# A new table of durations, a term for changes of matmul kind and other begin and due times in the planner of a linear-attention and MLP kernel

## The chip, the cores and the metric

The kernel runs on one core of one Trainium2 chip. The metric is device microseconds (us) of one execution. Of the kernel before, three runs were timed; one more execution was taken by the hardware profiler, and everything read from a trace comes from that one.

## What is computed

The input is four arrays `r`, `k`, `v`, `w` of shape (4 batches, 8 heads, 768 tokens, 48 channels), a vector `u` per head, and the two weights of an MLP. All is float32. The attention is a recurrence over tokens with a 48x48 state per head:

```python
for t in range(S):
    cur = np.einsum('bhd,bhe->bhde', u[None] * kt, vt)
    y[:, :, t] = np.einsum('bhd,bhde->bhe', rt, state + cur)
    state = wt[:, :, :, None] * state + np.einsum('bhd,bhe->bhde', kt, vt)
```

The 8 heads of `y` are put side by side (384 columns, 3072 tokens). Then comes the MLP: `h = x @ w_in` (384 by 2048), an ELU, and `@ w_out` (2048 by 384).

## The kernel before

**Tiling.** The 768 tokens are cut into 6 chunks of 128. A chunk of one batch is a *unit*, so there are 24 units, numbered chunk by chunk: units 0 to 3 are chunk 0. The four units of a chunk give the 512 columns of one MLP pass. Chunks 2 to 4 (units 8 to 19) treat each unit as two half chunks of 64 tokens.

**Attention of a unit i.** Names in brackets are those of the planner. SyncE (SP) loads w, k, r, v and, from unit 8 on, rk (`ld_...`). VectorE (DVE) runs two scans over the decays (`es` L377, `gs` L387) and multiplies them into r and k (`rh` L392, `kh` L396). TensorE (PE) computes scores (`s` L456), transposes k (`t` L465), multiplies values (`v` L501, or L493 and L506 in half chunks), forms the outer product for the state (`u` L532) and, for half chunks, the part of the first half that comes from the state (`ya` L506). The diagonal term with `u` goes for units 0 to 7 through DVE (`rkc` L416), PE (`pd` L421) and ScalarE (ACT: the copy `md` L425, then eight instructions `sp` L432 that write the diagonal matrices); from unit 8 on through GpSimd (POOL: L404, L407, L442) and DVE (L411). DVE masks the scores (`mk` L460), scales and updates the state (`sc` L472, `up` L540 or L542). ACT copies the transposed k (`kt` L469), sums a flag (`fl` L401) and rounds the result to the upper part of x (`xh` L513); DVE takes the rest (`xl` L519).

**MLP.** Every product is made of three matmuls (upper by upper, lower by upper, upper by lower part). Its step n works on one block f of 128 hidden channels: `g1` (nine matmuls, L238), `r1`, `r2`, `gh` on ACT (L243, L246, L253), `stt` and `gl` on DVE (L249, L257), `g2` (nine matmuls, L268). In chunks 0 and 1 the first six blocks are done for the first two units and then for the last two (steps 0 to 5 and 6 to 11, each with half the columns); the other blocks and chunks take 512 columns at once. Chunk 0 has the steps 0 to 21, chunk 1 the steps 22 to 43, and every later chunk 16.

**Weights.** In the first part of the program the weights of block f are converted: `a` on ACT (L559), `cand`, `cb`, `cc` on DVE (L563, L567, L571), `wh` on ACT (L574), `wl` on DVE (L577). `g1` of block f in chunk 0 needs `wl` of f.

**What sets the order.** Every engine runs its instructions in the order in which they are written, and `Plan` (L76 and below) writes them. Every task has an engine, a duration from the table `COST` (L54), tasks before it, pool slots it must hold, and sometimes a due time, which comes from `BEGINS` (when each chunk's MLP should begin), `STAG` and `STAG_C`. From the due times a latest start is worked back for every task. Then the planner plays the program through with its durations: whenever an engine is free, it takes of the ready tasks the one with the earliest latest start. `BEGINS` less `LEAD` is also the earliest time at which it lets a chunk's loads be issued. PSUM has one pool `pa` of three buffers, taken in turn, for all attention products: a task that writes into one waits until the task that read it three buffers earlier is done. So the score of a unit with the diagonal on PE, which takes two of them, waits for the `md` copies of the two `pd` ahead of it.

```python
late = [ts[s_]["late"] - ts[s_]["dur"] - LAT - (DMA_LAT if t["eng"] == "SP" else 0) for s_ in succ[k]]
u = (t["late"] + (STAY if e == "PE" and (k[0] in MODES) != (mode in MODES) else 0.0), rank[k])
end = now + t["dur"] * (2.0 if e == "PE" and now < HALF else 1.0)
```

Of the kernel before, what the change touches and what calls it, by code (L numbers as in the profile page):

```python
# [77 lines left out]
class Plan:  # L78
# [5 lines left out]
    def add(self, key, eng, dur, fn, after=(), due=None, start=0.0, lock=False, size=0):  # L84
        self.tasks[key] = dict(key=key, eng=eng, dur=dur, fn=fn, after=list(after), due=due, start=start, lock=lock, size=size)
# [8 lines left out]
    def order(self):  # L94
# [35 lines left out]
        while len(order) < len(ts):  # L130
            moved = False
            for e in ready:
# [159 lines left out]
def rwkv_elu_kernel(ctx, tc, wkr, rk, vp, u, uz, gkrw, gv, gu, w_in, w_out, out):  # L292
    nc = tc.nc
# [303 lines left out]
    for u_ in units:  # L597
# [258 lines left out]
```

## Time and profile before

| | |
|---|---|
| median of three runs | 541.37 us (541.27 to 541.45) |
| the profiled execution's own time | 543.14 us |
| its span, first to last instruction | 540.9 us |
| PE busy | 515.5 us (95% of the span) |
| DVE, ACT, POOL busy | 371.1, 285.8, 74.7 us |
| mean granted TensorE clock | 0.974 of full speed |

The span is the part of the execution that the trace covers; 2.2 us of the profiled execution lie outside it. That execution took 1.77 us more than the median of the runs shown, so a sum that is made on its trace is moved by that much to speak of the median. Busy time of PE includes matmuls that overlap, so a stretch in which PE is busy throughout can still hold short pauses. A granted clock of 0.5 is the lower of the two levels, 1.2 GHz, 1.0 the upper, 2.4 GHz.

### The profile page before, as it was taken

To read this page: it belongs to the slowest core of one execution; us is meant where nothing else is said; L and a number is where in the kernel's file an instruction comes from. 1 tells how busy PE (TensorE), PEld (TensorE's weight loads), DVE (VectorE), ACT (ScalarE), POOL (GpSimd) and SP (SyncE) were. 2 spreads that over 40 slices of the span, in tenths; PEclk is the share of its full clock that TensorE was granted. 3 is DMA by queue.
4 is the path that set the end of the run, shared out by engine and by line. 5 is a ranking of instruction groups with operands and counts; after the bars stand their busy time and mean duration, and the time that the engine had idled before them with its cause. 6 is when DMAs were issued, how large, how long until landed. Compare 5 with 4: busy or idle time off the path is not lost.

```text
span 540.9 us, 12202 instructions
## 1 busy us (share of the span) xinstructions
PE 515.5 (95%) x5121; PEld 427.7 (79%) x5121; DVE 371.1 (69%) x614; ACT 285.8 (53%) x570; POOL 74.7 (14%) x102
## 2 busy tenths in 40 slices
PE   6876999989999999999999999999999999999994
PEld 5666998878999777787777788777788887888883
DVE  5899899988778875469964478964436995333331
ACT  3768588675855453455453365543355543454441
POOL 2000000000243120028120035120031400000000
PEclk9977899979999999999999999999999999999998
DMA  8954754021562200094310083100084110010001
GB/s 243 287 176 141 226 175 164 19 56 35 175 178 76 65 2 2 2 263 133 85 33 2 3 241 103 35 2 3 1 254 124 48 35 2 0 60 0 1 0 63
DMA packets 26749, 47.54 MB, mean 88 GB/s; under 512 B 2753, under 2 KB 9281, under 8 KB 26689
## 3 DMA queue, kind: packets, MB, share of 16 engines
q1 hardware_dynamic: 26544, 46.58, 28.7%
q8 instruction: 42, 0.69, 0.5%
q14 instruction: 19, 0.15, 0.1%
q10 hardware_dynamic: 144, 0.13, 0.1%
HBM read 41.98 MB, written 4.72 MB: 86 GB/s over the span
## 4 chain that ended last, share of the span: by engine, by line
PE 80%; DVE 9%; DMA 6%; ACT 2%; issue 1%; SPq 0%; DVEq 0%; ACTq 0%
PE ph L238 34%; PE acc L268 33%; PE pa_s L456 3%; PE pa_y L501 3%; DMA v<-in_vp_dram 3%; PE pa_u L506 2%; PE pa_u L493 2%; PE pa_u L532 1%; DMA wrawx<-in_w_out_dram 1%; DMA rk<-in_rk_dram 1%; PE pa_t L465 1%; DVE eg L387 1%; DVE gl L257 1%; DMA k<-in_wkr_dram 1%; DVE r L392 1%
## 5 line engine op out<-in xcount | busy, mean ns | idle before, releaser
L243 ACT ACTIVATE m<-ph 128x512 f32<-128x512 f32 (+1 forms) x108 | 59.2, 549 | 132.8 <-PE ph L238 131.5
L249 DVE SCALAR_TENSOR_TENSOR m<-m,ph 128x512 f32<-128x512 f32 (+1 forms) x108 | 67.4, 624 | 84.7 <-ACT m L246 84.2
L238 PE MATMUL ph<-xh,w_h 128*128 128x512 f32 (+1 forms) x324 | 123.2, 380 | 2.0 <-ACT w_h L574 1.6
L238 PE MATMUL ph<-xh,w_l 128*128 128x512 f32 (+1 forms) x324 | 120.7, 372 | 3.7 <-DVE w_l L577 3.7
L268 PE MATMUL acc<-gh,w_h 128*128 128x512 f32 (+1 forms) x325 | 123.6, 380 | 0.0
L268 PE MATMUL acc<-gl,w_h 128*128 128x512 f32 (+1 forms) x325 | 120.2, 370 | 0.1
L238 PE MATMUL ph<-xl,w_h 128*128 128x512 f32 (+1 forms) x324 | 120.1, 371 | 0.0
L268 PE MATMUL acc<-gh,w_l 128*128 128x512 f32 (+1 forms) x325 | 119.9, 369 | 0.0
L257 DVE TENSOR_TENSOR gl<-m,gh 128x512 fp32r<-128x512 f32 (+1 forms) x108 | 73.2, 681 | 36.4 <-ACT gh L253 35.9
L253 ACT CAST gh<-m 128x512 fp32r<-128x512 f32 (+1 forms) x108 | 61.5, 571 | 55.9 <-DVE m L249 33.2
L238 PEld LDWEIGHTS ph<-xh,w_l 128*128 128x128 f32 x324 | 62.3, 192 | 15.0 <-DVE w_l L577 4.6
L238 PEld LDWEIGHTS ph<-xh,w_h 128*128 128x128 f32 x324 | 62.2, 192 | 14.3 <-ACT w_h L574 2.4
L268 PEld LDWEIGHTS acc<-gh,w_h 128*128 128x128 f32 x325 | 62.4, 192 | 12.8 <-issue 1.0
L268 PEld LDWEIGHTS acc<-gh,w_l 128*128 128x128 f32 x325 | 62.4, 192 | 10.2
L268 PEld LDWEIGHTS acc<-gl,w_h 128*128 128x128 f32 x325 | 62.5, 192 | 9.7 <-DVE gl L257 0.5
L238 PEld LDWEIGHTS ph<-xl,w_h 128*128 128x128 f32 x324 | 62.5, 193 | 9.4
L246 ACT ACTIVATE m<-m 128x512 f32<-128x512 f32 (+1 forms) x108 | 63.3, 586 | 2.9
L442 POOL TENSOR_SCALAR_AFFINE_SELECT am<-md 64x256 f32<-64x256 f32 (+1 forms) x56 | 30.5, 548 | 96.9 <-PE pa_u L493 61.9
L404 POOL TENSOR_TENSOR rk<-rk 128x384 f32<-128x384 f32 x16 | 19.1, 1192 | 134.1 <-DMA rk<-in_rk_dram 132.2
L377 DVE TENSOR_TENSOR_SCAN eg<-w,reset 112x516 f32<-112x516 f32 (+1 forms) x24 | 31.0, 1292 | 2.6 <-DMA w<-in_wkr_dram 2.6
L456 PE MATMUL pa_s<-r,k 48*64 48x64 f32 (+1 forms) x576 | 27.3, 262 | 5.5 <-ACT md L425 2.2
L401 ACT ACTIVATE junk<-eg,lim 112x1032 bf16<-112x1032 f32 (+1 forms) x24 | 27.7, 1153 | 8.2 <-DVE eg L387 8.2
(72 smaller groups left out, 513.4 us busy)
## 6 DMA issues: line engine op xcount, KB each, us to landing
v<-in_vp_dram SPq DMA_DIRECT2D x24, 256.0 KB, 6.5
rk<-in_rk_dram SPq DMA_DIRECT2D x16, 384.0 KB, 4.1
w<-in_wkr_dram SPq DMA_DIRECT2D x24, 227.9 KB, 3.9
k<-in_wkr_dram SPq DMA_DIRECT2D x24, 224.0 KB, 4.9
r<-in_wkr_dram SPq DMA_DIRECT2D x24, 224.0 KB, 5.3
out_dram<-o SPq DMA_DIRECT2D x17, 256.0 KB, 2.5
wrawx<-in_w_in_dram SPq DMA_DIRECT2D x10, 384.0 KB, 3.5
wrawx<-in_w_out_dram SPq DMA_DIRECT2D x10, 384.0 KB, 4.1
```

Of the source, the lines that this page charges most:

```text
L238: nc.tensor.matmul(ph[z:z + COLS], w[:, f, 0, k, z:z + COLS], x_[:, k, :], start=(k == n == 0), stop=(k == NK - 1 and n == 2))
L243: act(s["m"], s["ph"], AF.Relu, scale=-1.0)
L246: act(s["m"], s["m"], AF.Exp, scale=-1.0)
L249: stt_(s["m"], s["m"], -1.0, s["ph"], ALU.add, ALU.max)
L253: nc.scalar.copy(s["gh"], s["m"])
L257: nc.vector.tensor_tensor(s["gl"], s["m"], s["gh"].bitcast(F32), ALU.subtract)
L268: nc.tensor.matmul(a_[z:z + COLS], w[:, f, 1, m, z:z + COLS], g[:, s_], start=(f == n == 0 and lo == 0), stop=(f == NF - 1 and q == parts ...
L377: nc.vector.tensor_tensor_scan(out=eg[:, 0, 0:n][:, ::-1], data0=u_["w"][:, 1:n + 1][:, ::-1], data1=reset[:, 0, 0:n][:, ::-1], initial=0. ...
L401: act(junk[:, :, 0:n], u_["eg"][:, :, 0:n], AF.Relu, bias=lim, accum_out=flags[:, u_["i"]:u_["i"] + 1])
L404: eng.tensor_tensor(u_["rk"][:, 0], u_["rk"][:, 0], u_["rk"][:, 1], ALU.mult)
L442: nc.gpsimd.affine_select(out=am[rs, :, 0:L], in_=u_["md"][rs, q::2].unsqueeze(2).broadcast_to([L, NP, L]), pattern=[[0, NP], [1, L]], com ...
L456: nc.tensor.matmul(pa[q][ts, p, 0:L], u_["k"][rs, p, ts], u_["r"][rs, p, ts], start=True, stop=True)
```

## The change

No instruction is added, removed or given another shape: only the planner's inputs and one of its rules change, so each engine and each queue gets the same instructions in another order. `COST` has other durations (most are shorter; `pd` is 0.95 instead of 0.6, and `u` of a half chunk has an entry of its own). `BEGINS` has other times. `HALF` makes every PE task that the planner starts before 17.0 us count twice. `SWITCH` adds 0.1 us where two PE tasks of different kinds follow each other, and the new `OUTSIDE` 0.08 us where PE goes between attention and MLP; both lengthen the planner's PE tasks but do not enter its choice among ready tasks. `STAG` and `STAG_C` move the due times of the values. `conv_n` and `conv_d` are never called, since `BY_DMA` is empty.

```diff
-COST = dict(es=1.5, gs=1.4, pc=0.2, pd=0.6, md=0.22, spa=2.4, rh=0.62, kh=0.62, rk=0.48, rku=0.48, prk=1.1, prku=1.1, dg=0.5, mk=0.7, up=0.7, sc=0.5, xl=0.48,
...
+COST = dict(es=1.3, gs=1.45, pc=0.15, pd=0.95, md=0.15, spa=2.4, rh=0.61, kh=0.61, rk=0.48, rku=0.48, prk=1.0, prku=1.1, dg=0.48, mk=0.65, up=0.72, sc=0.48, xl=0.48,
...
-BEGINS = (20.9, 120.4, 207.5, 284.8, 361.5, 453.5, 461.1)
+BEGINS = (14.3,130.1,206.5,308.7,373.1,470.3,477.5)
 SOON = 0.0
-HALF = 0.0
-STAY = 0.0
-SWITCH = 0.0
-MODES = dict(s=1, v=2, u=3, pd=4)
-STAG = 10.9
-STAG_C = 0.0
+HALF = 17.0
+STAY = 0
+SWITCH = 0.1
+MODES = dict(s=1, v=2, ya=2, u=3, pd=4, t=5)
+OUTSIDE = 0.08
+STAG = 10
+STAG_C = 8
+BY_DMA = ()
...
                 if e == "PE":
-                    end += SWITCH * (MODES.get(mode, 0) != MODES.get(k[0], 0))
+                    end += SWITCH * (MODES.get(mode, 0) != MODES.get(k[0], 0)) + OUTSIDE * ((mode in MODES) != (k[0] in MODES))
                     mode = k[0]
...
+    def conv_n(f):
+        act(w_l[:, f], w_h[:, f].bitcast(F32), AF.Copy, scale=-1.0)
+
+    def conv_d(f):
+        nc.gpsimd.dma_start(w_l[:, f].bitcast(F32), raws[f][1].bitcast(F32), accum_op=ALU.add)
...
-            add(("u", i), "PE", K["u"], lambda u_=u_: outer(u_), [("kt", i)] + after[:3])
+            add(("u", i), "PE", K["uh"], lambda u_=u_: outer(u_), [("kt", i)] + after[:3])
...
-        add(("wl", f), "DVE", K["wl"], lambda f=f: conv_l(f), [("wh", f)], lock=True)
+        if f in BY_DMA:
...
+        else:
+            add(("wl", f), "DVE", K["wl"], lambda f=f: conv_l(f), [("wh", f)], lock=True)
```

**Where the order changes.** ACT at the start of the program, from its first conversion on. The rows are `a` 0, `fl` 0 and what follows (`wg` is the conversion's tile, `junk` that of `fl`, `am` the diagonal matrices). Before:

```order
L559 ACTIVATE wg<-wraw 128x768
L401 ACTIVATE junk,flags<-eg,lim 112x2x516
L425 COPY md<-pa_d 128x8
L432 ACTIVATE am<-ident,md 128x128 x8
L425 COPY md<-pa_d 128x8
L469 COPY kt<-pa_t 128x448
L432 ACTIVATE am<-ident,md 128x128 x8
L559 ACTIVATE wg<-wrawx 128x768
L401 ACTIVATE junk,flags<-eg,lim 112x2x516
L574 CAST w_h<-wg 128x768
L513 CAST xh<-pa_y 128x3x128
L559 ACTIVATE wg<-wrawx 128x768
```

With the change:

```order
L561 ACTIVATE wg<-wraw 128x768
L403 ACTIVATE junk,flags<-eg,lim 112x2x516
L561 ACTIVATE wg<-wrawx 128x768
L403 ACTIVATE junk,flags<-eg,lim 112x2x516
L576 CAST w_h<-wg 128x768
L427 COPY md<-pa_d 128x8
L434 ACTIVATE am<-ident,md 128x128 x8
L427 COPY md<-pa_d 128x8
L434 ACTIVATE am<-ident,md 128x128 x8
L471 COPY kt<-pa_t 128x448
L576 CAST w_h<-wg 128x768
L561 ACTIVATE wg<-wrawx 128x768
```

The second conversion, the flag of unit 1 and the first `w_h` now stand ahead of the two diagonal copies `md` with their `sp`; before, both `sp` stood ahead of them.

DVE at the border of chunk 0 and chunk 1, from the last `cc` (L571) to the masks of unit 4. `eg` is written by the scans, `gl` is step 19 of the MLP, `st<-pa_u` the state update of unit 3. Before:

```order
L571 SCALAR_TENSOR_TENSOR wg<-wraw,wg 128x768
L249 SCALAR_TENSOR_TENSOR m<-m,ph 128x512
L386 RECIPROCAL reset<-eg 112x4
L387 SCALAR_TENSOR_TENSOR eg<-w,reset 112x516
L377 SCALAR_TENSOR_TENSOR eg<-w,reset 112x516
L542 COPY st<-pa_u 48x4x48 x2
L392 TENSOR_TENSOR r<-r,eg 112x512
L396 TENSOR_TENSOR k<-k,eg 112x512
L577 TENSOR_TENSOR w_l<-wg,w_h 128x768
L257 TENSOR_TENSOR gl<-m,gh 128x512
L460 COPY_PREDICATED am<-upper,pa_s 128x512 x2
```

With the change, from the first scan of unit 4 (`L379`, L377 before) on:

```order
L379 SCALAR_TENSOR_TENSOR eg<-w,reset 112x516
L418 TENSOR_TENSOR rkc<-r,k 112x512
L585 TENSOR_TENSOR w_l<-wg,w_h 128x768
L259 TENSOR_TENSOR gl<-m,gh 128x512
L388 RECIPROCAL reset<-eg 112x4
L389 SCALAR_TENSOR_TENSOR eg<-w,reset 112x516
L379 SCALAR_TENSOR_TENSOR eg<-w,reset 112x516
L394 TENSOR_TENSOR r<-r,eg 112x512
L398 TENSOR_TENSOR k<-k,eg 112x512
L388 RECIPROCAL reset<-eg 112x4
L389 SCALAR_TENSOR_TENSOR eg<-w,reset 112x516
L394 TENSOR_TENSOR r<-r,eg 112x512
```

The last `w_l` and `gl` 19 now stand ahead of the second scan of unit 4 and the first of unit 5, and the state update of unit 3 stands behind the first two masks.

PE at the same border: the diagonals of units 4 and 5 (`pa_d`), the outer product of unit 3 (`pa_u`), the scores of units 4 and 5 (`pa_s`), `g2` 19 (`acc`) and `g1` 21 (`ph`). Before:

```order
L421 MATMUL pa_d<-ubd,rkc 128x2 x8
L532 MATMUL pa_u<-v,kt 48x48 x8
L456 MATMUL pa_s<-r,k 128x128 x8
L238 MATMUL ph<-xh,w_h 128x512
L238 MATMUL ph<-xl,w_h 128x512
```

With the change (each line of dots is the rest of a group of nine):

```order
L423 MATMUL pa_d<-ubd,rkc 128x2 x8
L270 MATMUL acc_442<-gh,w_h 128x512
L270 MATMUL acc_442<-gl,w_h 128x512
...
L240 MATMUL ph<-xh,w_h 128x512
L240 MATMUL ph<-xl,w_h 128x512
...
L458 MATMUL pa_s<-r,k 128x128 x8
L534 MATMUL pa_u<-v,kt 48x48 x8
L458 MATMUL pa_s<-r,k 128x128 x8
L503 MATMUL pa_y<-r,st 32x128 x12
```

`g2` 19 and `g1` 21 now stand between the diagonals and the score of unit 4; before, they came after it.

## Rows read from the trace of the kernel before

**Rows 1.** The profile cut at seven places of the program (busy time by stretch): start:end, length, busy us of PE, PE's weight load, DVE, ACT and POOL with the number of instructions, granted clock, DMA share, GB/s.

```profile
0.00:26.69 26.69, 19.39 (x172) 16.87 (x172) 18.85 (x32) 13.70 (x31) 2.79 (x10) 1.00 0.96 268
26.69:63.31 36.62, 28.77 (x240) 25.20 (x236) 33.84 (x55) 24.32 (x54) 0.00 (x0) 0.77 0.52 168
63.31:108.09 44.78, 44.78 (x255) 39.46 (x254) 43.69 (x67) 33.76 (x60) 0.00 (x0) 1.00 0.41 135
108.09:127.31 19.22, 17.04 (x209) 14.65 (x207) 15.69 (x26) 13.25 (x33) 0.00 (x0) 0.82 0.24 63
127.31:177.39 50.08, 50.08 (x510) 46.00 (x507) 40.20 (x74) 32.55 (x84) 14.46 (x18) 1.00 0.38 116
177.39:306.41 129.02, 128.54 (x1865) 101.17 (x1864) 89.26 (x161) 59.27 (x116) 25.92 (x34) 1.00 0.22 62
306.41:533.50 227.09, 226.94 (x1887) 184.32 (x1885) 128.31 (x201) 108.71 (x195) 31.56 (x40) 1.00 0.18 54
```

**Rows 2.** The same view for three shorter stretches, with the granted clock of TensorE in the third column from the right.

```profile
31.40:38.30 6.90, 5.50 (x25) 4.91 (x24) 6.71 (x11) 4.87 (x10) 0.00 (x0) 0.51 0.63 207
51.90:58.80 6.90, 6.36 (x56) 5.39 (x57) 5.73 (x12) 2.41 (x6) 0.00 (x0) 0.51 1.04 321
113.40:120.20 6.80, 5.55 (x24) 4.62 (x25) 5.96 (x10) 4.09 (x14) 0.00 (x0) 0.50 0.17 41
```

**Rows 3.** Timeline of ACT, 12 to 24 us (columns: start us, us, engine, line, operation, written<-read, shape, count, and in brackets the idle time before it and what ended it).

```profile
12.70 2.45 ACT L432 ACTIVATE am<-ident,md 128x128 f32<-128x128 f32 x8
15.05 0.14 ACT L425 COPY md<-pa_d 128x8 f32<-128x8 f32 x1
15.10 0.52 ACT L469 COPY kt<-pa_t 128x448 f32<-128x448 f32 x1
15.52 2.45 ACT L432 ACTIVATE am<-ident,md 128x128 f32<-128x128 f32 x8
20.37 0.91 ACT L559 ACTIVATE wg<-wrawx 128x768 f32<-128x768 f32 x1 [2.40 <-DMA wrawx<-in_w_out_dram]
21.19 1.14 ACT L401 ACTIVATE junk<-eg,lim 112x1032 bf16<-112x1032 f32 x1
22.33 0.81 ACT L574 CAST w_h<-wg 128x768 fp32r<-128x768 f32 x1
23.05 0.46 ACT L513 CAST xh<-pa_y 128x384 fp32r<-128x384 f32 x1
```

**Rows 4.** Timeline of PE near 20 us, same columns: the end of the score of unit 1 and the value product of unit 0.

```profile
18.47 2.07 PE L456 MATMUL pa_s<-r,k 48*128 48x128 f32 x14 [1.14 <-DVE am L460]
20.47 1.93 PE L501 MATMUL pa_y<-am,v 128*32 128x128 f32 x32
```

**Rows 5.** Timeline of DVE, 26 to 62 us, same columns.

```profile
26.81 0.72 DVE L542 COPY st<-pa_u 48x192 f32<-48x192 f32 x2
30.77 0.95 DVE L571 SCALAR_TENSOR_TENSOR wg<-wrawx,wg 128x768 uint32<-128x768 uint32 x1
38.82 0.69 DVE L416 TENSOR_TENSOR rkc<-r,k 112x512 f32<-112x512 f32 x1
40.89 1.23 DVE L377 TENSOR_TENSOR_SCAN eg<-w,reset 112x516 f32<-112x516 f32 x1
42.81 1.23 DVE L377 TENSOR_TENSOR_SCAN eg<-w,reset 112x516 f32<-112x516 f32 x1
57.73 0.56 DVE L519 TENSOR_TENSOR xl<-pa_y,xh 128x384 fp32r<-128x384 f32 x1 [1.17 <-ACT xh L513]
61.19 0.42 DVE L249 SCALAR_TENSOR_TENSOR m<-m,ph 128x256 f32<-128x256 f32 x1 [1.23 <-ACT m L246]
```

**Rows 6.** Timeline of PE, 114 to 124 us, same columns: score of unit 4, the first matmul of `g1` 21, the first of `g2` 19, score of unit 5.

```profile
114.65 2.08 PE L456 MATMUL pa_s<-r,k 48*128 48x128 f32 x16 [2.18 <-ACT md L425]
116.66 0.79 PE L238 MATMUL ph<-xh,w_h 128*128 128x512 f32 x1
120.45 0.39 PE L268 MATMUL acc<-gh,w_h 128*128 128x512 f32 x1
123.02 1.16 PE L456 MATMUL pa_s<-r,k 48*128 48x128 f32 x16
```

**Rows 7.** Timeline of ACT near 113.7 us, same columns: the copy of the diagonal of unit 5.

```profile
113.67 0.14 ACT L425 COPY md<-pa_d 128x8 f32<-128x8 f32 x1
```

**Rows 8.** Timeline of PE at five places after 180 us, same columns: the outer products (L532) of units 8, 12 (in two pieces) and 16, and between them the state part of unit 12 (L506).

```profile
180.79 0.57 PE L532 MATMUL pa_u<-v,kt 64*48 64x48 f32 x32
258.42 0.29 PE L532 MATMUL pa_u<-v,kt 64*48 64x48 f32 x4
258.88 0.56 PE L532 MATMUL pa_u<-v,kt 64*48 64x48 f32 x28 [0.17 <-DVE am L460]
262.39 0.54 PE L506 MATMUL pa_u<-r,st 112*32 112x64 f32 x24 [0.19 <-DVE st L472]
340.42 1.00 PE L532 MATMUL pa_u<-v,kt 64*48 64x48 f32 x32
```

**Rows 9.** The instruction groups of DVE by line, all 24 of L396: busy us, mean ns of one, idle before.

```profile
L396 DVE TENSOR_TENSOR k<-k,eg 112x512 f32<-112x512 f32 x24 | 17.8, 741 | 0.0
```

**Rows 10.** Timeline of DVE near 253 us, columns as in rows 3: one of the 24.

```profile
253.12 1.50 DVE L396 TENSOR_TENSOR k<-k,eg 112x512 f32<-112x512 f32 x1
```

**Rows 11.** Timeline of POOL at the same time, same columns.

```profile
252.75 1.33 POOL L407 TENSOR_TENSOR rk<-rk,ub 128x384 f32<-128x384 f32 x1
```

More of the change, by code (lines that the diff above doesn't have):

```diff
@@ L51 @@
 PIECES = _pieces()
-COST = dict(es=1.5, gs=1.4, pc=0.2, pd=0.6, md=0.22, spa=2.4, rh=0.62, kh=0.62, rk=0.48, rku=0.48, prk=1.1, prku=1.1, dg=0.5, mk=0.7, up=0.7, sc=0.5, xl=0.48,
-            cand=0.5, cv=0.9, wl=0.9, stt=0.6, gl=0.64, fl=1.4, kt=0.5, xh=0.46, a=0.87, wh=0.8, r1=0.58, r2=0.6, gh=0.6,
-            sp=1.7, s=1.15, t=0.5, v=1.75, v0=1.1, u=0.5, g=2.06, out=0.6, sh=0.6, ya=0.4, vh=1.0)
+COST = dict(es=1.3, gs=1.45, pc=0.15, pd=0.95, md=0.15, spa=2.4, rh=0.61, kh=0.61, rk=0.48, rku=0.48, prk=1.0, prku=1.1, dg=0.48, mk=0.65, up=0.72, sc=0.48, xl=0.48,
+            cand=0.5, cv=0.88, wl=0.88, stt=0.6, gl=0.62, fl=1.2, kt=0.45, xh=0.45, a=0.83, wh=0.75, r1=0.57, r2=0.57, gh=0.55,
+            sp=1.6, s=0.95, t=0.4, v=1.6, v0=0.95, u=0.4, uh=0.45, g=2.045, out=0.6, sh=0.55, ya=0.38, vh=0.9)
 LAT = 0.06
 DMA_FIRST, DMA_ISSUE, DMA_LAT, DMA_RATE = 1.0, 0.45, 1.9, 215.0
-BEGINS = (20.9, 120.4, 207.5, 284.8, 361.5, 453.5, 461.1)
+BEGINS = (14.3,130.1,206.5,308.7,373.1,470.3,477.5)
 SOON = 0.0
-HALF = 0.0
-STAY = 0.0
-SWITCH = 0.0
-MODES = dict(s=1, v=2, u=3, pd=4)
-STAG = 10.9
-STAG_C = 0.0
+HALF = 17.0
[6 more added lines that the diff above has]
+BY_DMA = ()
 HALVES = (2, 3, 4)
@@ L117, in order @@
         free = lambda p, n: not any(ring[p][1][(ring[p][0] + x) % len(ring[p][1])] for x in range(n))
-        ready = {e: [] for e in ("PE", "DVE", "ACT", "POOL", "SP")}
+        ready = {e: [] for e in ("PE", "DVE", "ACT", "POOL", "SP", "NET")}
         count = {k: len(t["after"]) for k, t in ts.items()}
@@ L665, in rwkv_elu_kernel @@
         add(("wh", f), "ACT", K["wh"], lambda f=f: conv_h(f), [("cc", f)])
-        add(("wl", f), "DVE", K["wl"], lambda f=f: conv_l(f), [("wh", f)], lock=True)
+        if f in BY_DMA:
+            add(("wn", f), "ACT", 0.75, lambda f=f: conv_n(f), [("wh", f)])
+            add(("wd", f), "POOL", 1.0, lambda f=f: conv_d(f), [("wn", f)])
+            add(("wl", f), "NET", 4.5, lambda: None, [("wd", f)])
+        else:
+            add(("wl", f), "DVE", K["wl"], lambda f=f: conv_l(f), [("wh", f)], lock=True)
     n0, prev = 0, None
```

## The prediction, made before the changed kernel was run

> **What bounds the kernel now.** I read the stretches first [rows 1]. From 63.31 us on PE is busy throughout, at full clock, except in 108.09 to 127.31, where 17.04 of 19.22 us are busy and the clock is 0.82. Before 63.31 it is busy for 19.39 of 26.69 and 28.77 of 36.62 us, and DVE for 33.84 of those 36.62: the weight conversions on DVE set the pace there. So the order of the work can win or lose time in the first 63 us and at the border of chunks 0 and 1; elsewhere it can only remove or add short waits. Then the clock: it stood at about 0.5 in three stretches [rows 2], behind thin PE work before 31.4, around a wait before 52, and around the border. Then the timelines of ACT, DVE and PE at those places [rows 3 to 7].
>
> Instructions and shapes are the same, so all terms are waits and the clock. The sum is made on the profiled execution (543.14 us) and then moved by the 1.77 us by which this lies above the median of the runs shown.
>
> **Part 1: the start (to the first `g1` of the second half, PE at 63.31).** ACT now has `a` 1, `fl` 1 and `wh` 0 ahead of `md` 0. `a` 1 waited until 20.37 for its weights to land, 2.40 us behind ACT's last work [rows 3]; their load has the same place in its queue, up to a swap of the first two, so it lands no sooner. With 0.91 for `a`, 1.14 for `fl` and 0.81 for `wh`, overlapping a little, ACT is free at 23.05, where it began `xh` before [rows 3]. So `md` 0 comes at 23.05, `sp` 0 takes 2.45, and `md` 1 comes at 25.6; it came at 15.05 [rows 3]. The score of unit 0 waits for `sp` 0, and its second tile for the buffer that `md` 1 frees. With 2.07 for a score at this clock [rows 4] it ends at 27.7. The score of unit 1 takes the buffer that `kt` 0 frees: 25.7 plus 2.45 for `sp` 1 plus 0.52 is 28.7, and with 2.07 it ends at 30.8. The value product of unit 0 (1.93 [rows 4]) ends at 32.7. On DVE `xl` 0 follows at about 33.3, and `xl` 1 stands behind a `cand`, a `wl`, a `cb` and a `cc` (the long ones 0.95 [rows 5]) and an `up` (0.72): it ends at about 38.4. Before, `up` 1 behind it began at 26.81 [rows 5].
>
> Not all of these 11.6 us are lost, since DVE has meanwhile done other conversions, one `rkc` (0.69) and two scans (1.23 each), which came at 38 to 44 before [rows 5]. All it has done by then was done at 31.7 before (end of `cc` 2 [rows 5]), plus 3.15 for those three and less 0.72 for an `up` not yet done: 34.2. **DVE is 4.2 us behind.** From there on it has the same work. The order before lost 1.17 and 1.23 us in two DVE waits at 57.7 and 61.2 [rows 5]; the new one can have none. So the least cost is 4.2 - 2.4 = +1.8. Against it stands the clock: a stretch of 6.9 us at 0.51 costs 3.4 us if PE is what bounds in it [rows 2]. In the new order `g1` 3 waits for `wl` 3 and `g1` 5 for `wl` 5, by the DVE times above about 3.3 and 2.7 us; the wait at the border before (2.18 [rows 6]) was one behind which the clock fell. The last blocks before the second half can thus run at 0.5, and the first `g1` of the second half itself at half clock costs up to 0.75. Most is 1.8 + 3.4 + 0.75 = +5.9. I take +3.7, near the middle: PE has some slack against DVE there, so part of the half clock is hidden. The nearest row says the same, 28.77 busy of 36.62 at a mean clock of 0.77.
>
> **Part 2: 63 to 108.** PE is busy in 44.78 of 44.78, DVE in 43.69 [rows 1]. Work is exchanged between DVE tasks there, but `gl` stays ahead of its `g2` by 0.4 to 3 us in the order that I worked through with the rows' durations. I take 0; if that cover goes, DVE's share says that it becomes the bound, at up to the same 1 us.
>
> **Part 3: the border.** PE waited 2.18 us before the score of unit 4 until `md` 5 was copied (113.67, in the timeline of ACT [rows 6, 7]). Behind that wait the score took 2.08 instead of the 1.16 that the next one took (0.92 too much), and `g1` 21 took from 116.66 to 120.45, 3.79 where nine full-clock matmuls take 2.14 (1.65 too much) [rows 6]. The order now puts `g2` 19 and `g1` 21, about 4.1 us of PE work, between the diagonals and that score, so `md` 5 is copied beside them, PE has no pause and the clock no reason seen in these rows to fall. That is 2.18 + 0.92 + 1.65 = **-4.75**. A new wait: `v` of unit 5 now needs that unit's masks sooner, with the second scan and the first of unit 5 also ahead on DVE, +0.9 (0 to 1.2: a mask and a half of DVE work at most, as the two scans of 1.23 [rows 5] can be late by one).
>
> **Part 4: 127 to 177.** `u` 6 now stands right behind `t` 6 and so waits for `kt` on ACT, 0.52 [rows 3] and a hand-over: +0.6. DVE's scans and POOL's first diagonals now lie closer together. How that bears on PE isn't shown where PE is busy 50.08 of 50.08, so +0.6 to +2.0; I take +0.8.
>
> **Part 5: 177 to 306 and unit 16.** The outer products of half chunks took 0.57 for 32 [rows 8]. That of unit 12 came in two pieces, from 258.42 to 259.44 (1.02), with 0.17 of wait, that of unit 16 took 1.00, and the state part waited 0.19. If the new order has none of these waits, 0.45 + 0.43 + 0.19 = -1.1. The units 12 to 15 stand closer together now, with margins of about 0.3 us to DVE and POOL, so new waits of the same kind may come: up to +0.9, two like those. I take -0.4. `kh` is an example of what crowds: it took 1.50 us while POOL ran a product at the same time, against a mean of 0.741 [rows 9 to 11].
>
> The new terms for changes of kind move the planner's clock, not the chip's: 58 runs of attention and MLP work on PE become 57, which I cost at nothing. Sum: +3.7 + 0 - 4.75 + 0.9 + 0.8 - 0.4 = +0.25, which is **543.4 on the profiled execution and 541.6 as a median**.
>
> **Rivals.**
> A, *faster*: the start costs only the 1.8 at which DVE's lag and its own two waits stand, because PE's half clock is hidden behind DVE (as it was in most of 26.69 to 63.31, with DVE busy 33.84 of 36.62), and the small waits after 177 go. 1.8 - 4.75 + 0.9 + 0.6 - 1.1 = -2.55: 538.8. Against it: two PE waits of about 3 us ahead of the last half-width blocks.
> B, *slower*: at the start the clock stays at half over all of the last blocks before the second half, so PE, not DVE, ends that part. +5.9 there and the rest as forecast, 5.9 - 4.75 + 0.9 + 0.8 - 0.4 = +2.45: 543.8. It decides from the point where the start costs more than 3.45 + 1.1 = 4.5, that is when more than 2.7 of the 4.15 us of clock cost lie on the path. For it: the clock did fall behind waits of this size [rows 2, 6].
> C, *slower*: DVE and POOL slow each other. Where POOL's L407 took 1.33, `kh` took twice its mean [rows 9 to 11], and the new order puts POOL work of units 8 and 12 to 15 beside DVE's scans. With 0.75 more for each of two or three such operations ahead of a PE task, part 4 costs +2.0 and part 5 +0.9: 3.7 - 4.75 + 0.9 + 2.0 + 0.9 = +2.75: 544.1. Against it: the `md` and masks after 177 mostly have slack, as PE is busy 128.54 of 129.02.
> The Trainium skill, page "SBUF — State Buffer", section "Who interferes with whom", has the rule behind this: the two engines share a pair of ports that one instruction holds to its end, so that a DVE operation with two inputs in SBUF and a GpSimd operation that reads SBUF exclude each other. By that rule the waiting one pays the whole of the other's time, 1.33 here, which the measured 1.50 - 0.74 = 0.76 doesn't reach.
> D, the change does not do what it says: `HALF` and the new durations move work whose waits DVE hides at the start, and the border's wait only moves to the next unit. One change of kind less is then all, about the 0.2 of one of the short waits [rows 8]: 541.2, no change that could be told.
>
> **How the numbers follow.** Forecast 0.34, A 0.33, B 0.18, C 0.11, D 0.04. A measurement of this kernel can tell about 0.2% (1.1 us) from no change. A is faster; the forecast and D are within that; B and C are slower: 0.33, 0.38, 0.29. The range reaches from A less the 0.9 of the border's new wait (537.9, put at 537.8) to C plus the same 0.9 (545.0). The likeliest case alone has 540.5 to 542.7.
>
> **What would show it.** Part 1 is right if `md` 0 stands at about 23 us on ACT, the first score ends at 27 to 28, `xl` 1 at about 38, and the first `g1` of the second half starts at 65 to 69, at 67 by the forecast; the granted clock between 57 and 67 tells A from B. Part 3 is right if PE has no wait before the score of unit 4, the clock is 1.0 at 113 to 120 in that place, and the `g2` that began at 127.31 [rows 1] comes 3 to 5 us sooner against the second half's start than before. Part 4: a wait of 0.6 before `u` 6. Part 5: the outer products of units 12 and 16 at 0.57. The prediction is wrong if the start costs less than 2.6 or more than 4.8, or if the border keeps its wait.

## The result, and the profile after

The change is **slower**: 546.81 us median of five runs (545.50 to 548.20) against 541.45 for before; the ratio is 1.0093, with a 95% interval of 1.0066 to 1.0120, so +5.0 us. That is above the range of the forecast (537.8 to 545.0). The profiled execution took 548.20 us (span 546.3), 5.06 more than that of before.

First the stretches of the changed kernel, cut at the same tasks as [rows 1]: first `g1` (35.16; before 26.69), first `g1` of the second half (66.41; before 63.31), `g2` 18 (111.18; before 108.09), `g2` 20 (130.93; before 127.31), and last the `g2` of step 35 (184.70). Columns as in [rows 1]; the last row is a shorter stretch at a lower clock.

```profile
0.00:35.16 35.16, 18.98 (x165) 16.61 (x165) 24.81 (x37) 16.47 (x40) 2.79 (x10) 1.00 0.75 227
35.16:66.41 31.25, 26.06 (x233) 24.07 (x233) 28.21 (x49) 21.06 (x45) 0.00 (x0) 0.78 0.32 102
66.41:111.18 44.77, 43.56 (x256) 37.38 (x255) 41.78 (x66) 33.52 (x59) 0.00 (x0) 1.00 0.59 183
111.18:130.93 19.75, 18.51 (x214) 15.61 (x212) 18.49 (x29) 13.07 (x34) 0.00 (x0) 0.91 0.17 51
130.93:184.70 53.77, 51.88 (x550) 47.34 (x547) 44.40 (x78) 34.10 (x87) 15.20 (x18) 1.00 0.37 112
57.30:64.20 6.90, 6.90 (x97) 6.00 (x96) 4.61 (x12) 2.52 (x6) 0.00 (x0) 0.70 0.01 2
```

PE is no longer busy throughout from 66 to 111 (43.56 of 44.77; it was 44.78 of 44.78), and has pauses from 131 to 185 (51.88 of 53.77). Some tasks lie on other sides of these cuts now (`g1` 20 behind `g2` 18, `g2` 5 ahead of `g1` 6), so I also worked the loss out by task: for each PE task the time from its start to the next task's start, less the usual step of its kind (the value that a fifth of the steps of that kind, over all traces here, stay below), added up by stage. A wait thus stands with the task ahead of it. The sums differ between two kernels by just as much as their last PE task ends apart. For the change against before: **start +2.9, 63 to 108 us +2.8, border -1.6, 127 to 177 +2.1, 177 to 306 -0.3, rest -0.7: +5.2.**

Start: ACT and PE of the change, columns as in [rows 3].

```profile
18.99 0.89 ACT L561 ACTIVATE wg<-wrawx 128x768 f32<-128x768 f32 x1 [6.96 <-DMA wrawx<-in_w_out_dram]
20.92 0.82 ACT L576 CAST w_h<-wg 128x768 fp32r<-128x768 f32 x1
21.64 0.16 ACT L427 COPY md<-pa_d 128x8 f32<-128x8 f32 x1
24.24 0.14 ACT L427 COPY md<-pa_d 128x8 f32<-128x8 f32 x1
```

```profile
24.44 2.07 PE L458 MATMUL pa_s<-r,k 48*128 48x128 f32 x14 [1.79 <-ACT md L427]
27.33 2.08 PE L458 MATMUL pa_s<-r,k 48*128 48x128 f32 x16 [0.82 <-ACT kt L471]
```

ACT now stands 6.96 us at the weights of block 1, and begins with them at 18.99, 1.4 us sooner than in [rows 3] (two other traces with the start of before, e7 and e16, have 19.18 and 19.34, so the one of [rows 3] was late). `md` 0 comes at 21.64 and `md` 1 at 24.24, the first score ends at 26.5, the second waits for `kt`. Each is the row that the forecast worked out, earlier by 1.2 to 1.4.

PE and DVE further on in the start: PE at the last block of the first half, then DVE at `xl` 1 and at the masks of unit 3.

```profile
55.98 0.58 PE L240 MATMUL ph<-xh,w_l 128*128 128x256 f32 x1 [2.25 <-DVE w_l L585]
```

```profile
36.09 0.56 DVE L521 TENSOR_TENSOR xl<-pa_y,xh 128x384 fp32r<-128x384 f32 x1
61.71 1.35 DVE L462 COPY_PREDICATED am<-upper,pa_s 128x512 f32<-128x512 uint32 x2 [2.08 <-PE pa_s L458]
```

PE waits 2.25 us for the last `wl` of the first half and then has no pause until 66.41, with the clock at 0.5 up to 61.46. DVE waits 2.08 for the score that PE computes in that time.

From 63 to 108 us, the queue of SP (the second number is the time to issue), and then the row on ACT, on DVE and on PE that waited in turn:

```profile
75.73 0.38 SPq L556 DMA_DIRECT2D wrawx<-in_w_in_dram  x1
77.14 0.33 SPq L373 DMA_DIRECT2D k<-in_wkr_dram  x1
78.39 0.35 SPq L373 DMA_DIRECT2D r<-in_wkr_dram  x1
79.08 0.35 SPq L373 DMA_DIRECT2D v<-in_vp_dram  x1
79.93 0.35 SPq L556 DMA_DIRECT2D wrawx<-in_w_out_dram  x1
```

```profile
87.18 0.89 ACT L561 ACTIVATE wg<-wrawx 128x768 f32<-128x768 f32 x1 [3.04 <-DMA wrawx<-in_w_out_dram]
```

```profile
88.10 0.56 DVE L565 TENSOR_SCALAR wrawx<-wrawx 128x768 uint32<-128x768 uint32 x1 [2.34 <-ACT wg L561]
```

```profile
90.31 0.50 PE L240 MATMUL ph<-xh,w_h 128*128 128x512 f32 x1 [0.91 <-DVE m L251]
```

The two halves of the weights of block 11 are issued 4.2 us apart, since the loads of k, r and v of unit 6 stand between them in SP's queue, and each issue waits. What it waits for, by the view of SP's waits from 77 to 80.4 us (us in total, times, longest):

```profile
SPq L373 <- DMA w<-in_wkr_dram: 1.0, 1, 1.0
SPq L373 <- DMA wrawx<-in_w_out_dram: 0.9, 1, 0.9
SPq L556 <- DMA r<-in_wkr_dram: 0.5, 1, 0.5
SPq L373 <- DMA k<-in_wkr_dram: 0.3, 1, 0.3
```

So these loads wait for no buffer, though the expectation of e2 below says so. Each of the four issues waits until the load eight places ahead in the queue has landed (the program counts landings with eight semaphores, taken in turn). Each load that stands ahead of the second half costs it 0.7 to 1.3 us here. ACT waits 3.04 us for the second half, DVE 2.34 for ACT, and PE 0.91, with a shorter wait of 0.23 before `g2` 18.

The border, PE and then DVE:

```profile
121.83 1.16 PE L458 MATMUL pa_s<-r,k 48*128 48x128 f32 x16
122.92 0.56 PE L534 MATMUL pa_u<-v,kt 128*48 128x48 f32 x16
124.37 1.76 PE L458 MATMUL pa_s<-r,k 48*128 48x128 f32 x16 [0.89 <-DVE am L462]
126.06 1.32 PE L503 MATMUL pa_y<-r,st 112*32 112x128 f32 x24
128.85 1.27 PE L503 MATMUL pa_y<-r,st 112*32 112x128 f32 x24
```

```profile
123.00 0.68 DVE L251 SCALAR_TENSOR_TENSOR m<-m,ph 128x512 f32<-128x512 f32 x1
123.59 1.33 DVE L462 COPY_PREDICATED am<-upper,pa_s 128x512 f32<-128x512 uint32 x2
```

The waits of PE's weight load from 122.5 to 127 us (us in total, times, longest), and two stretches with columns as in [rows 1], the score of unit 5 and the time at half clock:

```profile
PEld pa_s L458 <- DVE am L462: 1.3, 2, 1.0
```

```profile
124.37:126.06 1.69, 1.56 (x16) 1.26 (x16) 1.64 (x4) 1.69 (x4) 0.00 (x0) 1.00 0.48 155
126.31:129.72 3.41, 3.41 (x74) 3.40 (x69) 2.55 (x5) 0.71 (x4) 0.00 (x0) 0.50 0.24 67
```

The score of unit 4 has no wait and takes 1.16, as the forecast said (it waited 2.18 and took 2.08 [rows 6]). The next score waits 0.89 for the first mask of unit 4, which stands behind `stt` 20 on DVE. It waits a second time within its 1.76, for the second mask: the clock is 1.00 over this score, so the 0.6 by which it is longer than 1.16 is not the clock. **Behind these two waits the clock falls**, from 126.31 to 129.72: the value product of unit 4 takes 2.79 from start to next start where 1.65 is usual, and that of unit 5 takes 2.08. By steps, the two waits cost 0.95 + 0.60 and the half clock 1.14 + 0.43.

From 127 to 177: PE at `u` 6 and `t` 7, then DVE, then POOL at the same time:

```profile
162.78 0.56 PE L534 MATMUL pa_u<-v,kt 128*48 128x48 f32 x16 [0.62 <-ACT kt L471]
164.52 0.57 PE L467 MATMUL pa_t<-ident,k 112*128 112x112 f32 x4 [1.18 <-DVE st L542]
```

```profile
160.44 1.37 DVE L474 TENSOR_TENSOR st<-st,pc 112x384 f32<-112x384 f32 x1
161.73 2.03 DVE L379 TENSOR_TENSOR_SCAN eg<-w,reset 112x520 f32<-112x520 f32 x1
163.69 0.69 DVE L542 TENSOR_TENSOR st<-st,pa_u 48x192 f32<-48x192 f32 x2
```

```profile
160.07 1.32 POOL L409 TENSOR_TENSOR rk<-rk,ub 128x384 f32<-128x384 f32 x1
161.36 1.31 POOL L406 TENSOR_TENSOR rk<-rk 128x384 f32<-128x384 f32 x1
162.74 1.81 POOL L409 TENSOR_TENSOR rk<-rk,ub 128x384 f32<-128x384 f32 x1
```

`u` 6 waits 0.62 for `kt`, as forecast. Then `t` 7 waits 1.18 for a state update that stands behind a scan of 2.03 us; its usual time is 1.23 ([rows 5]). Beside it POOL worked.

### The profile page after: what moved, and what is told of

Its sections match the earlier page's. It is cut to its first block, busy times and chain, and to the rows that moved or that the text cites. A ratio compares the mean times of both kernels' runs of the same rounds, so it can differ in the third digit from the quotient of the medians.

```text
span 546.3 us, 12213 instructions
## 1 busy us (share of the span) xinstructions
PE 511.9 (94%) x5121; PEld 425.4 (78%) x5121; DVE 369.2 (68%) x614; ACT 286.8 (52%) x570; POOL 77.0 (14%) x102
## 4 chain that ended last, share of the span: by engine, by line
PE 77%; DVE 11%; DMA 7%; ACT 3%; issue 2%; SPq 0%; ACTq 0%; DVEq 0%
PE acc L270 33%; PE ph L240 32%; PE pa_s L458 3%; PE pa_y L503 3%; DMA wrawx<-in_w_out_dram 3%; DMA r<-in_wkr_dram 2%; PE pa_u L508 2%; PE pa_u L495 2%; DVE wg L569 2%; DVE w_l L585 2%; ACT am L434 1%; PE pa_u L534 1%; DVE gl L259 1%; DVE m L251 1%; DMA v<-in_vp_dram 1%
## 5 line engine op out<-in xcount | busy, mean ns | idle before, releaser
L458 PE MATMUL pa_s<-r,k 48*64 48x64 f32 (+1 forms) x576 | 26.2, 257 | 12.3 <-ACT md L427 9.3
L458 PEld LDWEIGHTS pa_s<-r,k 48*64 48x64 f32 (+1 forms) x576 | 21.6, 163 | 18.2 <-ACT md L427 10.0
L379 DVE TENSOR_TENSOR_SCAN eg<-w,reset 112x516 f32<-112x516 f32 (+1 forms) x24 | 31.5, 1311 | 4.2 <-DMA w<-in_wkr_dram 4.2
```

What stands on the lines that cost most here:

```text
L379: nc.vector.tensor_tensor_scan(out=eg[:, 0, 0:n][:, ::-1], data0=u_["w"][:, 1:n + 1][:, ::-1], data1=reset[:, 0, 0:n][:, ::-1], initial=0. ...
L458: nc.tensor.matmul(pa[q][ts, p, 0:L], u_["k"][rs, p, ts], u_["r"][rs, p, ts], start=True, stop=True)
```

## The experiments

Each kernel ran on one chip together with runs of before, so its time is given as the ratio to before with its interval (0.002 is 1.1 us). The right half is the loss by PE task against before, in us, from each kernel's profiled execution.

| kernel | ratio (95%) | start | 63-108 | border | 127-177 | 177-306 | rest |
|---|---|---|---|---|---|---|---|
| the change | 1.0093 (1.0066-1.0120) | +2.9 | +2.8 | -1.6 | +2.1 | -0.3 | -0.7 |
| e1_start | 1.0029 (1.0010-1.0047) | -1.4 | +2.8 | -1.6 | +2.1 | -0.2 | -0.6 |
| e2_load | 1.0037 (1.0014-1.0060) | +2.9 | +1.0 | -3.3 | +2.1 | -0.2 | -0.6 |
| e3_masks | 1.0082 (1.0050-1.0115) | +3.5 | +2.6 | -3.6 | +2.1 | -0.3 | -0.7 |
| e4_up5 | 1.0089 (1.0060-1.0117) | +2.1 | +3.0 | -1.7 | +1.5 | -0.2 | -0.6 |
| e5_half | 1.0068 (1.0044-1.0092) | +4.5 | 0.0 | 0.0 | 0.0 | -0.3 | -0.1 |
| e6_begins | 1.0154 (1.0123-1.0185) | -2.3 | +2.5 | -3.1 | +4.2 | +1.5 | +6.7 |
| e7_border | 1.0012 (0.9987-1.0037) | -0.5 | 0.0 | -1.2 | +1.7 | -0.6 | -0.1 |
| e8_all | 1.0038 (1.0014-1.0063) | -0.1 | +2.4 | -1.8 | +1.4 | +3.3 | -0.7 |
| e9_act | 1.0152 (1.0127-1.0178) | +7.4 | 0.0 | -0.1 | 0.0 | -0.9 | -0.1 |
| e10_pool | 1.0117 (1.0096-1.0137) | +0.4 | +2.4 | -1.6 | +2.2 | -0.3 | -0.7 |
| e11_two | 1.0053 (1.0031-1.0075) | -0.5 | +3.1 | -1.6 | +2.1 | -0.3 | -0.7 |
| e12_four | 1.0009 (0.9987-1.0031) | -1.0 | +4.2 | -3.6 | +2.3 | -0.3 | -0.6 |
| e13_nohalf | 1.0241 (1.0203-1.0279) | -0.5 | +4.5 | -4.2 | +0.3 | +10.2 | +1.0 |
| e14_nohalf_load | 1.0196 (1.0154-1.0237) | -0.7 | +1.5 | -4.2 | +0.3 | +11.6 | +1.0 |
| e15_less_dve | 1.0058 (1.0037-1.0080) | +1.3 | +1.9 | -1.6 | +2.1 | -0.3 | -0.6 |
| e16_less_dve_before | 0.9994 (0.9972-1.0017) | -1.0 | 0.0 | -0.2 | 0.0 | -1.1 | 0.0 |
| e17_rest_before | 0.9992 (0.9971-1.0012) | -2.2 | +2.9 | -1.2 | +2.5 | -0.7 | -0.1 |
| e18_rest_after | 1.0051 (1.0033-1.0068) | -0.2 | +2.0 | -2.7 | +4.1 | -0.2 | -0.6 |

One execution's start is not one number: the six traces with the very start of the change lose 28.1 to 31.2 us there (mean 29.9), the three with that of before 26.8 to 27.7 (27.2). And since a wait stands with the task ahead of it, some waits are booked in a neighbouring stage: the wait before the score of unit 5 stands under 127-177 in e6 (1.8) and in e13, e14, e17 and e18 (0.9 each), because a task of that stage goes ahead of that score there, and in e8 the border column holds 1.9 of a wait behind `g2` 21.

**The start.** e1 and e9 run an explicit list of tasks, e5 changes one constant of before:

```diff
-HALF = 0.0
+HALF = 17.0
```

```diff
 ACT of e9, before with two tasks moved
+a.1 fl.1
 md.0 sp.0 md.1 kt.0 sp.1
-a.1 fl.1
```

> The changed kernel, with PE, DVE and ACT in the order of before up to the first g1 of the second half (g1 6); all loads and all later work in the changed order. Theory (the places add up): the start costs what the trace of the change shows, first g1 at 66.41 instead of 63.31, so this run is about 3 us faster than the change: 543.8 (542.8 to 544.8). Rival 1 (the start is hidden behind the weights that land late at 87 us, so the later wait grows by what the start gives): 546 to 547. Rival 2 (most of the loss comes from the start, also the later waits): 541.5 to 542.5.

> The kernel before with HALF = 17.0 alone. Its order differs from before in the first 40 us only: a 1 and fl 1 stand ahead of md 0 on ACT (wh 0 behind both sp), pd 2 ahead of the score of unit 1 on PE, and the masks behind the conversions on DVE. Theory (ACT held by the weights that land at 20 us makes the start late, and this term alone puts it there): 2 to 3 us slower than before, 545.3 on the scale of 542.8 for before. Rival (the conversions on DVE hide it, and the start of the change is slow for another reason): within 0.5 of before, 543.0.

> The kernel before with two rows moved on ACT alone: a 1 and fl 1 ahead of md 0. Nothing else changes, so DVE still has the masks of unit 0 ahead of cc 0 and must wait for them. Theory (the start's cost is ACT standing at the weights that land at 20 us, and the changed DVE order only covers a part of it): md 0 comes at about 22 instead of 12.5, the masks some 8 to 9 us later, and DVE has nothing else to do: 5 to 8 us slower than before, 549 on the scale of 542.5, more than the 3.6 that HALF alone cost. Rival (the start's cost comes from the order on DVE and PE, ACT is harmless): under 1 us.

All three came out on the side of the theory, e5 and e9 a little above its numbers. With the start of before the change is 3.5 us faster than it was; `HALF` alone, which moves nothing behind 45 us, costs before 3.7; and ACT's two rows alone cost 8.2, since DVE there has no other work ahead of the masks. So ACT's wait for the weights makes the start slow, and the rest of the order that `HALF` brings covers a half of it. DVE's part of that order, with conversions ahead of the masks, is the likely reason; it was not run apart.

**The load.** In e2, where the kernel walks the planner's list, one task is moved:

```diff
-        for t in plan.order():
-            t["fn"]()
+        seq = [t["key"] for t in plan.order()]
+        for k, a in [(('raw', 11, 1), ('ld_k', 6))]:
+            seq.remove(k)
+            seq.insert(seq.index(a), k)
+        for k in seq:
+            plan.tasks[k]["fn"]()
```

> The changed kernel with one load moved in SP's queue: the second half of the weights of block 11, which stands behind the loads of k, r and v of unit 6 and so waits for their buffers (issued 79.93, its first half 75.73), right behind its first half. Theory: ACT's wait of 3.04 for it at 87 goes, with it the PE wait of 0.91 and the short ones behind it (some 2.2 in all by the PE steps from 87 to 112): 544.6 (543.8 to 545.6). Rival (DVE is the bound there anyway, PE waits a little later for the next conversions): 546.4 to 547.2.

It is 3.0 us faster than the change, by one load. In its trace SP issues the second half right behind the first, ACT's long wait is gone, and PE at the border shows the same waits with another clock behind them:

```profile
75.67 0.38 SPq L556 DMA_DIRECT2D wrawx<-in_w_in_dram  x1
76.40 0.33 SPq L556 DMA_DIRECT2D wrawx<-in_w_out_dram  x1
77.89 0.33 SPq L373 DMA_DIRECT2D k<-in_wkr_dram  x1
```

```profile
80.12 0.92 ACT L561 ACTIVATE wg<-wrawx 128x768 f32<-128x768 f32 x1 [0.41 <-DMA v<-in_vp_dram]
```

```profile
122.49 1.77 PE L458 MATMUL pa_s<-r,k 48*128 48x128 f32 x16 [0.89 <-DVE am L462]
124.19 0.86 PE L503 MATMUL pa_y<-r,st 112*32 112x128 f32 x24
125.74 0.84 PE L503 MATMUL pa_y<-r,st 112*32 112x128 f32 x24
```

By the traces, 1.8 of the gain lie in the stretch from 63 to 108, where 1.0 of the change's 2.8 stay. Another 1.7 are at the border, where both waits stand (0.89, and a score of 1.77 at a clock of 1.00, as the row shows) but the value products ran at full clock too:

```profile
122.49:124.19 1.70, 1.57 (x17) 1.26 (x17) 1.66 (x4) 1.70 (x4) 0.00 (x0) 1.00 0.56 154
```

That part isn't the load's for certain: of the seven traces with this wait of 0.89 or 0.90 (the change, e1, e2, e4, e10, e11, e15), six have a value product of unit 4 of 2.8 to 2.9 from start to start, one (e2) has the usual one.

**The border.** e3 moves the masks (`mk.4.0` and `mk.4.1` ahead of `stt.20`) in the change. e7 puts the border into before. e15 and e16 leave out five `cb`, and with them the low bits of five blocks' weights, in the change and in before:

```diff
         for t in plan.order():
+            if t["key"][0] == "cb" and t["key"][1] >= 11:
+                continue
             t["fn"]()
```

> The changed kernel with the two masks of unit 4 moved ahead of stt 20 on DVE. Theory: the score of unit 5 waits 0.3 instead of 0.89, and the clock, which fell behind that wait (0.75 over 124.3 to 131), stays up: 0.6 + 0.6 + 1.1 + 0.4 = 2.7 faster, 544.1 (543.3 to 545.0). Rival 1 (the clock falls anyway, as PE still pauses there): only 0.6, 546.2. Rival 2 (stt 20 comes too late for gl 20 and g2 20): no gain, 546.8.

> The kernel before with the border alone in the order of the change (everything from g2 18 to g2 20 on all engines), and the masks of unit 4 ahead of stt 20. Theory: of the 5.2 us that the border lost before, 1.6 stay, as in the run with the masks moved: 3.6 faster than before, 539.2 on the scale of 542.8. Rival (the clock falls behind another pause, or DVE is late for g2 20): 541 to 542.

> The changed kernel without cb of the blocks 11 to 15 on DVE (5 of 0.95, 4.8 us of DVE work between 88 and 109); the low bits of those weights are left out, nothing else changes. Theory (DVE is the bound from the late load to the border): the waits of PE behind 90 us go, the 0.89 before the score of unit 5 and the clock's fall behind it with them: 3 to 4 faster than the change, 543 to 544. Rival (the order between ACT, PE and the load sets the waits): under 1.

> The kernel before, with the same five cb left out. Theory A (as the forecast had it: PE waits at the border for md 5, which hangs on PE's own order and ACT): no gain, within 0.5 of before, with the same 2.18 before the score of unit 4. Theory B (DVE bounds the border in this order too): 2 us or more faster.

e3's trace has the shorter wait and no half clock (wait 0.32, border -3.6 instead of -1.6; e12 has the same numbers), but its time can't be told from the change's. Its score of unit 5 still takes 1.76, at a clock of 1.00: the second 0.6 of the theory's sum is the wait for the second mask, and it stays. e7 missed: in before the work ahead of the border is not late, and PE comes there sooner against DVE (the mask begins 2.24 us behind the start of the score of unit 4, 1.19 in e3), so the same score waits 1.35 and the clock falls. The thought that DVE's share of work bounds the border fell with e15 and e16: with 4.8 us of DVE work less the wait of 0.90 and the fall behind it stay in the changed order (what e15 gains on the change, about 1.9 us with intervals that overlap, lies in the start and from 63 to 108), and the 2.18 before the score of unit 4 stays in the old one, which gained nothing. **The order of a few tasks sets these waits at the border, not the amount of work.**

In e13 the planner itself put the masks ahead of `stt` 20 and `u` 3 behind the value product. It has -4.2 at the border, or -3.3 with its wait of 0.65 before the score of unit 5, and no half clock. e14, e17 and e18 have the same PE order there and the same wait (0.64, 0.64, 0.65): behind it the clock fell in e17 and e18, and not in e13 and e14.

**127 to 177.** e4 moves `up.5` ahead of `es.9` on DVE, e10 `rk.10 rku.10` behind `sp.9` on POOL, both in the change.

> The changed kernel with the state update of unit 5 moved ahead of the scan of unit 9 on DVE. Theory: the transpose of unit 7 waits 1.18 for that update, which stands behind the scan of 2.03; the wait goes: 545.6 (545.2 to 546.2). Rival (the scan is then late and the next product waits for it, or for POOL): 546.5 to 547.2. POOL's L409 and L406 still run beside the scan: by the ports theory it takes about 2 us again wherever POOL reads, against 1.23 alone.

> The changed kernel with POOL's rk 10 and rku 10 moved behind sp 9, so that no POOL product runs beside DVE's scan of unit 9. Theory (POOL's products slow DVE): that scan takes 1.2 to 1.3 instead of 2.03, PE's wait before the transpose of unit 7 falls from 1.18 to about 0.4; the time falls by 0.8, hardly more than a measurement can tell. The update sc 8 stays at 1.3 or more, since rku 9 still runs beside it. Rival (the scan is slow for its operands or its place): 2.0 again, no gain.

In time neither can be told from the change (e10's start was a short one, its median not). The traces decide the mechanism; of e10, on DVE, POOL and PE:

```profile
157.47 1.36 DVE L474 TENSOR_TENSOR st<-st,pc 112x384 f32<-112x384 f32 x1
158.76 1.23 DVE L379 TENSOR_TENSOR_SCAN eg<-w,reset 112x520 f32<-112x520 f32 x1
```

```profile
157.10 1.32 POOL L409 TENSOR_TENSOR rk<-rk,ub 128x384 f32<-128x384 f32 x1
```

```profile
160.75 0.57 PE L467 MATMUL pa_t<-ident,k 112*128 112x112 f32 x4 [0.39 <-DVE st L542]
```

Without POOL beside it the scan takes 1.23 instead of 2.03 and PE's wait 0.39 instead of 1.18; the scaling of the state, still beside L409, stays at 1.36. In e4 the scan began first and took 1.29, and POOL's L409, 1.0 alone, took 1.81 beside it: the one that comes second pays. This agrees with the Trainium skill, "SBUF — State Buffer", section "Who interferes with whom", which calls the port pair that the two engines share an exclusive lock and says that the order of issue decides who is blocked. In the stage as a whole nothing is gained: 127 to 177 is +2.2 in e10 (a `g2` at 172 us waits 0.42 for its `gl`, among others).

**Together.** e6 gives before the `BEGINS` of the change. e8, e11 and e12 put several places of the change right by an explicit list. e13 is the change with `HALF = 0.0`, e14 that with the load moved, e17 and e18 take e14's list up to `g2` 21 and the rest from before (e17) or from the change (e18).

> The kernel before with the BEGINS of the change alone. Start on ACT as before; g2 19 and g1 21 ahead of the score of unit 4; the loads of units 4 to 7 now among the weights of blocks 9 to 11. Theory (places add up): the border gives 3.3, the late loads cost 1.8 as they did in the change (PE waits near 85 to 90 us): 1.5 faster than before, 541.3 on the scale of 542.8. Rival 1 (the loads only hurt behind a late start): 539.5. Rival 2 (the loads cost more than the border gives): 543.5.

> The changed kernel with four places put right together: the start in the order of before, the load of block 11, the masks of unit 4, and the stretch from g2 21 to g2 35 in the order of before. Theory (places add up): 4.0 + 1.8 + 2.0 + 2.1 faster than the change (547.8 on the scale of 542.8 for before), which is 538.5 to 539.5, faster than before by 3 to 4. Rival (the wins overlap, since each removes the wait that the next would also have hidden): 541 to 543.

> The changed kernel with the start of before and the load of block 11 moved (and stt 6 ahead of cb 7, for the wait of 0.96 that the start of before brought). Theory (the change's loss is these two places, and they add up): 4.0 + 3.5 faster than the change, which stood 5.1 above before: 2.4 faster than before, 540.1 on the scale of 542.5. Rival 1 (they overlap, as the waits in the kernel with four places put right did): 542 to 543. Rival 2 (the border's clock falls again, by 2): 541.5 to 542.5.

> As the run before it, with the masks of unit 4 ahead of stt 20, the update of unit 5 ahead of the scan of unit 9, and rk 10 and rku 10 behind sp 9. Theory: 0.4 to 0.6 more at the border and 1.2 to 1.6 more from 127 to 177: 538.3 (537.5 to 539.5). Rival (each moved task makes another late, as in the kernel with four places put right): as the run before it, or slower.

> The change with HALF = 0.0, all other inputs as changed: the planner's own start, with md 0 ahead of a 1 on ACT, and the masks of unit 4 ahead of stt 20; the load of block 11 still behind the loads of unit 6. Theory (HALF puts the start late, by 3 to 4): 3.5 faster than the change, 543.5 on a scale of 542 for before. Rival (what DVE gains at the start it loses waiting for the late load and at the border): 545.5 to 547.

> As the run before it, with the load of block 11 moved ahead of the loads of unit 6. Theory: 2 to 3 faster than that run, as the load gave alone, 540.5 to 541.5, faster than before. Rival (the load only counts behind a late start): as that run, 543 to 544.

> To g2 21 the order of the run with HALF = 0 and the load moved (start as good as before, border without wait), from there the order of before. Theory (the loss of that run sits in the units 10 and 11 alone): waits and half clock of 1.3 to 108 us, 0.9 at the border, the rest as before: 3 to 3.5 faster than before, 538.5 on a scale of 542. Rival (the seam makes t 4 or what follows wait, with the clock behind it): 541 to 543.

> To g2 21 as the run before it, from there the order of the change, with the update of unit 5 ahead of the scan of unit 9 and rk 10 and rku 10 behind sp 9. Theory: as the run before it, plus 1 to 1.5 from 127 to 177 and less 0.7 to 1 behind 177: 538.5 to 539.5. Rival: 541 to 543, as there.

The theories of all eight missed on the slow side, and the table shows why: each wins where it was meant to and loses elsewhere. e6 wins the start and, with its wait of 1.57 before the score of unit 5, 1.3 at the border, and loses 6.7 behind 306 us, most of it behind one wait of 1.84 for a `gl` at 450 us. e8 waits 1.58 and 1.92 at the two seams of its stretch from `g2` 21 to `g2` 35. e11 waits 0.77 for an `stt` behind its hand-made start and loses as much from 63 to 108 as the change did. e13 loses 10.2 in units 10 and 11, whose products the new list puts side by side; beside such waits the clock is at 0.5 there from 225.15 to 238.80 (PE of e13):

```profile
229.25 0.88 PE L534 MATMUL pa_u<-v,kt 64*48 64x48 f32 x28 [0.48 <-DVE xl L521]
...
232.36 0.87 PE L508 MATMUL pa_u<-r,st 112*32 112x64 f32 x24 [1.43 <-DVE st L474]
```

e14 loses 1.4 more there than e13 and is still 2.4 us faster, though the two intervals overlap: with the load moved, ACT's wait of 4.88 and PE's of 1.52 near 85 us are gone, and 63 to 108 falls by 3.0. e12 is 2.4 us faster than e11, from which it differs at the border and behind it, and with all four places right it takes 4.5 us off the change. e12 and e17 come level with before. No version here beats it.

## Why the prediction was wrong

The trace has +5.2 where the sum had +0.25. By part, measured less forecast: -0.8, +2.8, +2.25, +1.3 and -0.6.

- **Part 1, the right chain, the size partly by luck.** Forecast +3.7; `HALF` alone 3.7, undoing the start 3.5, the one trace 2.9. The chain over `a` 1, `md`, score and `xl` 1 came as worked out, 1.2 to 1.8 us earlier (`xl` 1 at 36.6, forecast 38.4). By the forecast's own count DVE was thus 2.5 us behind (36.65 less its 34.2) and not 4.2. In return DVE has new waits, which the forecast put at none: 2.08 at 61.71 and 0.42 before. The half clock lay on the path in part, as taken: PE worked without a pause from 55.98, at 0.5 up to 61.46 (0.70 over 57.3 to 64.2), and the wait of 2.08 is for its score. The first `g1` of the second half ran at full clock.
- **Part 2, the step that failed.** The prediction took 0 from 63 to 108, measured +2.8; moving one load gives 1.8 of it back (e2), and the other 1.0 was not taken apart. The prediction looked at `gl` ahead of `g2` and at DVE's share, and not at SP's queue. That `BEGINS` less `LEAD` sets when a chunk's loads may be issued was known: for chunk 1, less 69.5, 60.6 instead of 50.9. That puts the loads of units 4 to 6 among the weights of blocks 10 and 11, issued at 70 to 80 us (the last of them at 63.57 before), and the second half of block 11 behind three loads that each wait for a landing.
- **Part 3, the right mechanism with its other half missing.** The old loss went as worked out: the score of unit 4, `g1` 21 and the wait ahead of them lost 4.9 in the trace of before by steps, and 0.1 in that of the change. The new wait was put at 0.9, before the value product of unit 5. It came before and within the score of unit 5, for both masks of unit 4, and cost 1.55. The half clock behind it, 1.57, was not in the sum: -1.6 instead of -3.85. A pause of 2.18 was taken as what makes the clock fall; the fall came behind 0.89 too, in six traces of seven, and behind 0.64 in two of four.
- **Part 4, mis-sized.** Forecast +0.8, measured +2.1, the upper bound and rival C's price. The wait for `kt` was right (0.62); the second, 1.18, is C's mechanism, though at one place and not in several. C's price of 0.75 fits as well (2.03 - 1.23 = 0.80). The prediction held the whole time of the other engine, 1.33, against it; but a product that begins second meets only what is left of the first: 0.96 left and 0.76 paid in [rows 10, 11], 0.94 left and 0.80 paid here.
- **Part 5.** Forecast -0.4, measured -1.0 with the rest: the outer products of units 12 and 16 take 0.57, as forecast, and a wait of 1.03 came. But five other traces with the order of before from 177 us on (e5, e7, e9, e16, e17) lose 0.4 to 1.1 less there than the one of before, so it isn't shown that the change gains anything here.
- **The rivals.** B's condition (a start over 4.5) did not come, C's price came in Part 4; none of them had the load. The range was too narrow because Part 2 had no bounds at all in the sum: "at up to the same 1 us" was said and not carried into it.

What stays open: whether the clock's fall at the border depends on more than chance (e2 against six others, e13 and e14 against e17 and e18), and how much of e2's 3.0 us is that. No run puts the loads of chunk 1 alone back to their times of before.

## What to carry to other kernels

When a planner's begin time moves, follow the load queue first: a load that waits, here for an earlier load to land, holds everything behind it, and the engine that suffers is several hand-overs away. When a long wait is removed, price the next one together with the clock behind it. And where one list orders everything, a win at one place is worth what is left of it after all later waits; place-by-place sums held in time for two single repairs of the list (e1, e2), could not be told for three (e3, e4, e10), and failed for every combination.

## What was not expected of the hardware

In the change PE had one pause of 0.23 us between 91 and 123 us, then waited 0.89 for a mask and once more for the next, and the clock was at half from 126.31 to 129.72. In six traces of seven such a pause was followed by half clock, in one not; with 0.64 it was two of four. The same start, instruction for instruction, lost between 28.1 and 31.2 us in six executions, so a start should be judged by times of many runs, not by one trace. And of two products on DVE and POOL at the same time, the one that came second took some 0.8 us longer (on DVE 2.03 for 1.23 and 1.37 for 0.56, on POOL 1.81 for 1.0).
